# Batch 1's pooled queries and keys summed by unit-matrix products, its pooled values summed inside the products that use them: a fused attention and feed-forward kernel

## The chip, the cores and the metric

The kernel runs on one core of one Trainium2 chip. The metric is the device time of one execution in microseconds (us). Three runs of the kernel before gave 1031.43, 1028.47 and 1034.59, a median of 1031.43. Engines are named as in the profile: PE is TensorE (PEld its weight loads), DVE is VectorE, ACT is ScalarE, POOL is GpSimd, SP is SyncE, which here issues most DMA transfers.

## The reference

Queries, keys and values have 8 batches, 8 heads, 576 positions and a head size of 64. Two attentions are added, and a gated feed-forward layer follows. In short:

```python
q_d, k_d, v_d = (t.reshape(B, H, Sd, 4, D).mean(axis=3) for t in (q, k, v))   # Sd = 144
out_up = np.repeat(sm_attn(q_d, k_d, v_d), 4, axis=2)                         # pooled attention
mask = np.abs(pos[:, None] - pos[None, :]) < 4                                # local attention
out_local = softmax(where(mask, q @ k.T / sqrt(D), -1e9)) @ v
x = (out_up + out_local) as 4608 tokens x 512
h = x @ w_in                                                                   # 512 -> 2048
return (h * cos(h)) @ w_out                                                    # 2048 -> 512
```

The pooled attention needs sums over four neighbouring positions of queries, keys and values; the change concerns these sums.

## The kernel before, in words

**Units.** The attention of one batch and one pair of heads is a unit; there are 32, four per batch. A unit runs in five functions. `u_qk` loads queries and keys with the head dimension on the partitions (128 x 584) and sums four neighbouring positions into `qkd` (128 x 144 each): by one DVE reduction (line 480) or three POOL additions (lines 473 and 475). `u_v` loads the values, once as `vd4` (72 x 8 x 128, where the eight are two halves of the pooled keys times four neighbours) for the pooled attention and once as `vl` for the local one, and sums `vd4` over its four neighbours into `vd` by two additions (lines 494 and 495) on POOL or DVE. `u_s` makes the local scores (96 matmul records, line 518) and the pooled scores (line 526), and runs both softmaxes: masks and maxima on DVE (537, 542, 550), exponentials on ACT (562, 565), sums and reciprocals on DVE (577 to 581), scaling on DVE or POOL (583). `u_t` transposes the weights, the local ones on DVE (600), the pooled ones on PE (609), with a copy from the accumulator bank by ACT or DVE (`evac`, 455 and 456). `u_pv` multiplies by the values: the pooled product on PE (626), the local product on PE (637). DVE joins the two into `xs` (645), and the sum is split into a high and a low part, `xh` (660 or 661) and `xl` (389), which are the feed-forward layer's inputs.

**Feed-forward.** Tokens go in 12 tiles of 384. For each tile and each of 16 chunks of 128 hidden columns, `gemm1` does 12 matmuls (line 688), ACT and DVE apply the gate (697 to 705), and `gemm2` does 9 matmuls two steps later (line 724). The first three tiles go through the chunks four at a time; the others take all 16 in a row. Tile 0 holds tokens of batch 0 only. Tile 1 (`x1h`, `x1l`) holds the rest of batch 0 and a third of batch 1, so its first `gemm1` can start only when all four units of batch 1 are done.

**Weights.** They arrive as 64-bit numbers in two words and are turned into a high and a low part by `w_split`: ACT (410), four DVE steps (411, 413, 415, 417), ACT or DVE (421, 422) and a subtraction on POOL or DVE (389).

**Order.** No engine's order is written by hand. The functions record operations with a due time, a cost and the buffers that they read and write; `Plan.schedule` goes over them eight times with its own costs and writes one order per engine, which the hardware then follows strictly. Operations with alternatives (a reduction on DVE or POOL, a copy on ACT or DVE) are placed by the same pass. Where the plan sees a gap on PE in the first 300 us, the last loop fills it with matmuls of a bf16 unit matrix (line 841, `ident_b`) that compute nothing that is used. Any change of a cost or an operation therefore moves other operations too. The loads are chained in a fixed order on SP.

**Names.** `early` is a unit of batch 0 or 1 (`NEARLY = 2`). `ON_PE` is a tuple, empty before. `ident` is the fp32 unit matrix. `wxi`, `wxo`, `xxl` and `xxh` in the profile are areas of later weights and tiles, lent to the early units' buffers and to `w_split`.

Of the kernel before, what the change touches and what calls it, by code (L numbers as in the profile page):

```python
# [36 lines left out]
SD = S // 4  # L37
# [9 lines left out]
F64_TOP = float(np.uint32(0x47EFFFFF).view(np.float32))  # L47
NEG = -2.0 ** 100
NEARLY = 2
ON_PE = ()  # L50
BOOST = {0: 100.0}
LAG = 2
PI = math.pi
# [246 lines left out]
def attn_ffn_kernel(ctx: ExitStack, tc: tile.TileContext, qT, kT, vdn, vl, w_in, w_out, out):  # L300
# [79 lines left out]
    def dma(nbytes, fn, r=(), w=(), pw=()):  # L380
        o = pl.op("SP", max(0.45, nbytes / 262e3), fn, r=r, w=w, pw=pw, lat=1.8)
        loads.setdefault((pl.name,) + pl.arg, []).append(o)
        return o
# [63 lines left out]
    def bank(b, kind):  # L447

        if b == 0:
            tags = ("pa.0", "po.0", "pa.1", "po.1") if kind == "s" else ("ph.0", "ph.1", "pa.2")  # L450
            return psum(tags[int(pl.turn("early" + str(kind == "s"), len(tags))[-1])])
        return psum(pl.turn("pa", 3))
# [6 lines left out]
    def u_qk(b, pr):  # L459
        pl.name = "u_qk"  # L460
        q, k, qkd = (ub(b, pr, n) for n in ("q", "k", "qkd"))
        s4 = [lambda: q.get()[:, 0:S].rearrange("p (a r) -> p a r", r=4), lambda: k.get()[:, PAD:PAD + S].rearrange("p (a r) -> p a r", r=4)]
        early = b < NEARLY
        bk = bank(b, "t") if early and ON_PE else None
        for i, (src, ram) in enumerate(((q, qT), (k, kT))):
            dma(4 * P * SP_, lambda src=src, ram=ram: sp.dma_start(src.get(), ram[b, pr]), w=[src])

            def on_pe(i=i):
                for r in range(4):
                    pe.matmul(bk.get()[:, i * SD:(i + 1) * SD], ident, s4[i]()[:, :, r], start=(r == 0), stop=(r == 3))  # L470

            def on_pool(i=i):
                pool.tensor_tensor(out=qkd.get()[:, i], in0=s4[i]()[:, :, 0], in1=s4[i]()[:, :, 1], op=ALU.add)
                for r in (2, 3):
                    pool.tensor_tensor(out=qkd.get()[:, i], in0=qkd.get()[:, i], in1=s4[i]()[:, :, r], op=ALU.add)
            if early and i in ON_PE:
                pl.op("PE", 4 * _mm4(SD), on_pe, r=[src], pw=[bk])
                evac(SD, lambda i=i: qkd.get()[:, i], lambda i=i: bk.get()[:, i * SD:(i + 1) * SD], bk, qkd)
            else:
                pl.op("DVE", _dve(S), lambda i=i: dve.tensor_reduce(out=qkd.get()[:, i], in_=s4[i](), axis=AX.X, op=ALU.add),  # L480
                      r=[src], pw=[qkd], alts=[("POOL", 3 * _pool(2 * SD), on_pool)])
        st[(b, pr)] = dict(q=q, k=k, qkd=qkd)

    def u_v(b, pr):
        pl.name = "u_v"
        vd4, vt = ub(b, pr, "vd4"), ub(b, pr, "vl")
        dma(16 * P * HD * 2, lambda: sp.dma_start(vd4.get(), vdn[b, pr].rearrange("p a r n -> p (a r) n")), w=[vd4])
        dma(4 * P * 12 * D, lambda: sp.dma_start(vt.get(), vl[b, pr]), w=[vt])
        vd = ub(b, pr, "vd")
        v4 = lambda: vd4.get().rearrange("p (a r) n -> p a r n", a=2)  # L490

        def v_add(e):
            def f():
                e.tensor_tensor(out=v4()[:, :, 0:2, :], in0=v4()[:, :, 0:2, :], in1=v4()[:, :, 2:4, :], op=ALU.add)
                e.tensor_tensor(out=vd.get(), in0=v4()[:, :, 0, :], in1=v4()[:, :, 1, :], op=ALU.add)
            return f
        pl.op("POOL", 2.2, v_add(pool), w=[vd, vd4], alts=[("DVE", 1.1, v_add(dve))], shares=True)
        st[(b, pr)].update(vd=vd, vl=vt)
# [116 lines left out]
    def u_pv(b, pr):  # L615
        pl.name = "u_pv"
        u = st.pop((b, pr))
        ptl, ptd, vd, vt = (u[n] for n in ("ptl", "ptd", "vd", "vl"))
        xd, xs = ub(b, pr, "xd"), ub(b, pr, "xs")
        banks = [bank(b, "v") for _ in range(2)]  # L620
        poo, loc = pl.buf(None), [pl.buf(None) for _ in banks]

        def d_mm():
            for kh in range(2):
                for h in range(2):
                    pe.matmul(banks[0].get()[64 * h:64 * h + 64, 2 * SD:3 * SD], vd.get()[:, kh, 64 * h:64 * h + 64],  # L626
                              ptd.get()[:, h, kh, :], start=(kh == 0), stop=(kh == 1))
        pl.op("PE", 0.64, d_mm, r=[vd, ptd], pw=[banks[0]], w=[poo])

        def l_mm():  # L630
            for a in range(NSEG // 2):
                for i in range(4):
                    for e in range(2):
                        for h in range(2):
                            r = slice(64 * h + 32 * e, 64 * h + 32 * e + 32)
                            o = (4 * a + i) * BQ
                            pe.matmul(banks[e].get()[64 * h:64 * h + 64, o:o + BQ], vt.get()[r, a, i, :], ptl.get()[r, 4 * a + i, :BQ],  # L637
                                      start=True, stop=True)
        pl.op("PE", 1.52, l_mm, r=[vt, ptl], pw=banks, w=loc)

        evac(SD, xd.get, lambda: banks[0].get()[:, 2 * SD:3 * SD], banks[0], xd, scale=0.25)
        xd.w[-1].deps += poo.w
        half = [pl.buf(None) for _ in range(2)]
        for e in range(2):
            pl.op("DVE", _dve(S // 2), lambda e=e: dve.tensor_tensor(
                out=xs.get().rearrange("p (a e n r) -> p a e n r", e=2, a=NSEG // 2, r=4)[:, :, e],
                in0=banks[e].get()[:, :12 * BQ].rearrange("p (a n r) -> p a n r", a=NSEG // 2, r=4),
                in1=xd.get().rearrange("p (a e n) -> p a e n", e=2, a=NSEG // 2)[:, :, e].unsqueeze(3).broadcast_to(
                    [P, NSEG // 2, BQ, 4]), op=ALU.add), r=[banks[e], loc[e], xd], pw=[xs], w=[half[e]])
        lo = 0  # L650
        while lo < S:

            tt = tile_of(b * S + lo)
            to = min(S, FROM[tt] + SIZE[tt] - b * S)
            a, m = b * S + lo - FROM[tt], to - lo
            written[tt] += m
            done = pl.buf(None)
            hi = lambda tt=tt, a=a, m=m: x_tile(tt)[0][:, pr, a:a + m]
            src = lambda lo=lo, to=to: xs.get()[:, lo:to]
            pl.op("ACT", _act(m, False), lambda hi=hi, src=src: act.activation(hi(), src(), AF.Copy),  # L660
                  r=[xs], w=[done], pw=[x_b[tt]], alts=[("DVE", _dve(m / 2), lambda hi=hi, src=src: dve.tensor_copy(hi(), src()))])
            sub(m, lambda tt=tt, a=a, m=m: x_tile(tt)[1][:, pr, a:a + m], src, lambda hi=hi: hi().bitcast(F32),
                r=[xs, done], pw=[x_b[tt]])
            lo = to
# [214 lines left out]
```

## Time and profile before

| what | value |
|---|---|
| runs | 1031.43, 1028.47, 1034.59 us |
| profiled execution | 1031.63 us, of which the span from the first to the last instruction is 1029.5 us |
| PE, PEld, DVE, ACT, POOL busy | 97%, 84%, 66%, 59%, 22% of the span |
| granted TensorE clock, mean | 0.983 |
| filler matmuls (line 841) | 124, in the first 112 us |
| first `gemm1` of tile 0, of tile 1 | 53.29 us, 115.32 us |

The profile is read as follows. A timeline row gives the start, the length, the engine, the line, the operation, what is written from what, how many records follow each other, and in brackets the engine's idle time before it with what ended that. A row of the chain of waits gives start, length and the engine and line on the path that ended last. An fp32 matmul stands as two records in the trace, so that the four matmuls of line 526 appear as x8. Consecutive DVE rows overlap by some 0.07 us, so that one costs that much less than its length when it stands in line. `issue` is time in which an engine waited for nothing that the profile shows.

### The profile page before, as it was taken

How to read it: one execution, taken by the hardware profiler on the slowest of the kernel's cores; microseconds unless marked ns; L12 is line 12 of the kernel's file. 1: busy time of each engine (PE TensorE's matmuls, PEld its weight loads, DVE VectorE, ACT ScalarE, POOL GpSimd, SP SyncE). 2: the span in 40 equal slices, each digit the busy share in tenths (PEclk: the TensorE clock that was granted, in tenths of full speed). 3: DMA queues.
4: the chain of work that ended last, by engine and by line, in shares of the span. 5: the costliest groups of instructions: out<-in, count | busy, mean ns of one | idle time of the engine just before them, and what ended most of it. 6: DMA issues, size and time to landing. Idle time of an engine off the chain costs nothing.

```text
span 1029.5 us, 25935 instructions
## 1 busy us (share of the span) xinstructions
PE 1003.0 (97%) x11068; PEld 864.9 (84%) x11068; DVE 676.9 (66%) x1353; ACT 610.6 (59%) x1176; POOL 228.8 (22%) x274
## 2 busy tenths in 40 slices
PE   7889999999999999999999999999999999999998
PEld 4557788889988888889898888888888888899997
DVE  6699889996478668564738856755646865543443
ACT  2546577786566666565646655655655765655554
POOL 5596424433135201010103300101002410000000
PEclk8988899999999999999999999999999999999999
DMA  9762751434245312100202401200101310000000
GB/s 265 237 221 85 242 183 46 61 59 62 32 106 144 76 50 75 59 25 28 76 6 76 133 28 38 96 25 28 55 27 43 120 51 1 32 1 1 31 1 31
DMA packets 36450, 76.11 MB, mean 74 GB/s; under 512 B 3440, under 2 KB 11632, under 8 KB 36336
## 3 DMA queue, kind: packets, MB, share of 16 engines
q1 hardware_dynamic: 32448, 67.38, 20.6%
q0 software_dynamic: 3888, 7.08, 5.0%
q8 instruction: 87, 1.43, 0.6%
q14 instruction: 27, 0.22, 0.1%
HBM read 57.93 MB, written 16.52 MB: 72 GB/s over the span
## 4 chain that ended last, share of the span: by engine, by line
PE 81%; DVE 10%; DMA 4%; ACT 2%; issue 2%; POOL 0%; SPq 0%; ACTq 0%; DVEq 0%; POOLq 0%
PE bank L688 35%; PE bank L724 35%; PE bank L637 3%; PE bank L518 3%; PE bank L526 2%; DMA q<-qT 2%; PE bank L609 2%; DMA wdi<-w_in 1%; PE bank L626 1%; DVE su L577 1%; DVE qkd L480 1%; DVE mxd L550 1%; PE bank L841 1%; DVE gl L389 1%; DVE tr L700 1%
## 5 line engine op out<-in xcount | busy, mean ns | idle before, releaser
L724 PE MATMUL bank<-wo,gh 128*128 128x512 f32 x1152 | 363.3, 396 | 0.0
L724 PEld LDWEIGHTS bank<-wo,gh 128*128 128x128 f32 x1152 | 210.0, 188 | 35.8 <-issue 2.3
L724 PE MATMUL bank<-wo,gl 128*128 128x512 f32 x576 | 228.0, 396 | 0.6 <-POOL su L535 0.6
L699 ACT ACTIVATE tr<-bank,bmagic 128x384 f32<-128x384 f32 x192 | 111.0, 579 | 134.0 <-PE bank L688 122.5
L703 DVE SCALAR_TENSOR_TENSOR tr<-tr,bank 128x384 f32<-128x384 f32 x192 | 105.3, 549 | 121.7 <-ACT tr L698 121.4
L700 DVE SCALAR_TENSOR_TENSOR tr<-tr,bank 128x384 f32<-128x384 f32 x192 | 105.5, 550 | 97.5 <-ACT tr L699 97.3
L697 ACT ACTIVATE tr<-tr 128x384 f32<-128x384 f32 x192 | 100.7, 524 | 84.4 <-DVE tr L700 83.7
L705 ACT ACTIVATE gh<-tr 128x384 fp32r<-128x384 f32 x177 | 92.5, 523 | 90.7 <-DVE tr L703 89.0
L389 DVE TENSOR_TENSOR gl<-tr,gh 128x384 fp32r<-128x384 f32 x160 | 97.3, 609 | 68.6 <-ACT gh L705 67.2
L724 PEld LDWEIGHTS bank<-wo,gl 128*128 128x128 f32 x576 | 108.0, 187 | 24.8 <-POOL su L535 1.0
L688 PE MATMUL bank<-x0h,wi 128*128 128x384 f32 x384 | 109.9, 347 | 0.7 <-DVE tr L703 0.7
L688 PE MATMUL bank<-x1h,wi 128*128 128x384 f32 x384 | 107.6, 341 | 0.0
L688 PE MATMUL bank<-x2h,wi 128*128 128x384 f32 x384 | 107.1, 339 | 0.0
L688 PE MATMUL bank<-x3h,wi 128*128 128x384 f32 x384 | 106.9, 339 | 0.0
L389 POOL TENSOR_TENSOR gl<-tr,gh 128x384 fp32r<-128x384 f32 x32 | 38.1, 1189 | 301.3 <-DVE gh L706 215.8
L698 ACT ACTIVATE tr<-tr 128x384 f32<-128x384 f32 x192 | 100.8, 525 | 6.1
L688 PEld LDWEIGHTS bank<-x0h,wi 128*128 128x128 f32 x384 | 72.1, 193 | 3.7 <-DVE tr L703 0.8
L688 PEld LDWEIGHTS bank<-x1h,wi 128*128 128x128 f32 x384 | 70.7, 189 | 2.9 <-issue 0.8
L688 PEld LDWEIGHTS bank<-x2h,wi 128*128 128x128 f32 x384 | 70.2, 188 | 2.8 <-DVE sml L537 0.6
L688 PEld LDWEIGHTS bank<-x3h,wi 128*128 128x128 f32 x384 | 70.2, 188 | 2.5 <-issue 0.6
L688 PE MATMUL bank<-x0l,wi 128*128 128x384 f32 x192 | 65.8, 342 | 0.0
L688 PE MATMUL bank<-x3l,wi 128*128 128x384 f32 x192 | 64.6, 336 | 0.5 <-POOL x3l L389 0.5
(192 smaller groups left out, 1473.0 us busy)
## 6 DMA issues: line engine op xcount, KB each, us to landing
vl<-vl SPq DMA_DIRECT2D x26, 384.0 KB
out<-ob SPq DMA_DIRECT2D x36, 256.0 KB
wdi<-w_in SPq DMA_DIRECT2D x16, 512.0 KB
wdo<-w_out SPq DMA_DIRECT2D x16, 512.0 KB
q<-qT SPq DMA_DIRECT2D x26, 292.0 KB
k<-kT SPq DMA_DIRECT2D x26, 292.0 KB
vd<-vdn SPq DMA_DIRECT2D x26, 288.0 KB
out<-ob POOLq DMA_DIRECT2D x27, 256.0 KB, 5.7
```

Of the source, the lines that this page charges most:

```text
L389: f = lambda e: lambda: e.tensor_tensor(out=out(), in0=in0(), in1=in1(), op=ALU.subtract)
L518: pe.matmul(banks[n // NSEG].get()[64 * h + BS * e:64 * h + BS * (e + 1), c:c + BS], q.get()[hs, o:o + BS], k.get()[hs, o:o + BS], start=T ...
L526: pe.matmul(banks[h].get()[:HD, i * SD:(i + 1) * SD], qkd.get()[hs, 0, i * HD:(i + 1) * HD], qkd.get()[hs, 1, :], start=True, stop=True)
L637: pe.matmul(banks[e].get()[64 * h:64 * h + 64, o:o + BQ], vt.get()[r, a, i, :], ptl.get()[r, 4 * a + i, :BQ], start=True, stop=True)
L688: pe.matmul(ph.get()[:, :m], w[:, i, kc, :], x[:, kc, :], start=(n == 0), stop=(n == 3 * KC - 1))
L697: act.activation(tr.get(), tr.get(), AF.Sin, scale=PI)
L698: act.activation(tr.get(), tr.get(), AF.Square)
L699: pl.op("ACT", _act(m, True, 1), lambda: act.activation(tr.get(), h(), AF.Identity, bias=bmagic), r=[ph], w=[tr])
L700: pl.op("DVE", _dve(m), lambda: dve.scalar_tensor_tensor(out=tr.get(), in0=tr.get(), scalar=MAGIC, in1=h(), op0=ALU.subtract, op1=ALU.subt ...
L703: pl.op("DVE", _dve(m), lambda: dve.scalar_tensor_tensor(out=tr.get(), in0=tr.get(), scalar=0.5, in1=h(), op0=ALU.subtract, op1=ALU.mult), ...
L705: pl.op("ACT", _act(m, False), lambda: act.activation(gh.get(), tr.get(), AF.Copy), r=[tr], w=[gh], alts=[("DVE", _dve(m / 2), lambda: dve ...
L724: pe.matmul(o, (gh, gh, gl)[k].get()[:, sl], wo.get()[:, (0, 1, 0)[k]], start=(c == c0 and k == 0), stop=(c == c1 - 1 and k == 2))
```

## The change

`ON_PE` becomes `(1,)` and now names batches. For the four units of batch 1:

- `u_qk` sums queries and keys on PE: four fp32 matmuls each with the stationary unit matrix and, as moving operand, every fourth position (`s4[i]()[:, :, r]`, a step of four elements), accumulated in a bank. Then `evac` copies the 128 x 144 result to `qkd`. Per unit that is 8 matmuls and two copies for two reductions (or six POOL additions).
- `u_v` ends after its loads; nothing sums the values. `u_pv` multiplies all eight slices of `vd4` instead of the two of `vd`, 16 matmuls in place of 4, each half of the weights used for its four neighbours. `vd4` stays in use until that product.

```diff
-ON_PE = ()
+ON_PE = (1,)
...
-        bk = bank(b, "t") if early and ON_PE else None
+        on = early and b in ON_PE
+        bk = bank(b, "t") if on else None
...
             def on_pe(i=i):
                 for r in range(4):
                     pe.matmul(bk.get()[:, i * SD:(i + 1) * SD], ident, s4[i]()[:, :, r], start=(r == 0), stop=(r == 3))
...
-            if early and i in ON_PE:
+            if on:
                 pl.op("PE", 4 * _mm4(SD), on_pe, r=[src], pw=[bk])
                 evac(SD, lambda i=i: qkd.get()[:, i], lambda i=i: bk.get()[:, i * SD:(i + 1) * SD], bk, qkd)
             else:
...
         dma(4 * P * 12 * D, lambda: sp.dma_start(vt.get(), vl[b, pr]), w=[vt])
+        if b in ON_PE:
+            st[(b, pr)].update(vd=vd4, vl=vt)
+            return
...
         def d_mm():
-            for kh in range(2):
+            n = 8 if b in ON_PE else 2
+            for j in range(n):
                 for h in range(2):
-                    pe.matmul(banks[0].get()[64 * h:64 * h + 64, 2 * SD:3 * SD], vd.get()[:, kh, 64 * h:64 * h + 64],
-                              ptd.get()[:, h, kh, :], start=(kh == 0), stop=(kh == 1))
-        pl.op("PE", 0.64, d_mm, r=[vd, ptd], pw=[banks[0]], w=[poo])
+                    pe.matmul(banks[0].get()[64 * h:64 * h + 64, 2 * SD:3 * SD], vd.get()[:, j, 64 * h:64 * h + 64],
+                              ptd.get()[:, h, j * 2 // n, :], start=(j == 0), stop=(j == n - 1))
+        pl.op("PE", 2.56 if b in ON_PE else 0.64, d_mm, r=[vd, ptd], pw=[banks[0]], w=[poo])
```

The planner's new order differs on every engine. The changed file is a few lines longer, so the same code has other numbers there: 471 is the unit product (470 before), 481 the reduction (480), 522 and 530 the local and pooled scores (518, 526), 546, 554 and 581 the maxima and sums (542, 550, 577), 613 the transposes on PE (609), 631 and 642 the pooled and local value products (626, 637), 693 and 729 the two feed-forward products (688, 724), 846 the filler (841); lines up to 455 are unchanged. Below, the changed numbers stand in the rows of the change; the text uses those of before.

The first place is PE from the pooled product of batch 0's third unit to the first `gemm1`. Before, with the filler rows left out where the dots stand:

```order
L626 MATMUL bank<-wxi_194 64x144 x4
...
L637 MATMUL bank<-wxo_384,wxi_496 64x24 x48
...
L609 MATMUL bank<-ident,wxi_208 72x72 x4
L518 MATMUL bank<-k,q 32x32 x48
...
L637 MATMUL bank<-wxi_550,wxo_579 64x24 x48
...
L626 MATMUL bank<-wxo_267 64x144 x4
...
L526 MATMUL bank<-qkd 72x144 x4
L688 MATMUL bank<-x0h,wi_936 128x384
```

The same place in the change (`xxl`, `wxo_787`, `wxi_799`, `wxo_826` and `wxo_841` are queries and keys of batch 1's other three units):

```order
L631 MATMUL bank<-wxi_194 64x144 x4
L471 MATMUL bank<-q,ident 128x144 x4
L471 MATMUL bank<-k,ident 128x144 x4
...
L613 MATMUL bank<-ident,wxi_208 72x72 x4
L471 MATMUL bank<-xxl,ident 128x144 x4
...
L471 MATMUL bank<-wxo_826,ident 128x144 x4
...
L631 MATMUL bank<-wxo_267 64x144 x4
...
L642 MATMUL bank<-wxi_544,wxo_579 64x24 x48
L471 MATMUL bank<-wxo_841,ident 128x144 x4
```

Seven of the eight groups of unit products now stand ahead of the last products of batch 0's fourth unit, the eighth behind them; the two score products of batch 1's first unit follow, and then two `gemm1` in a row (one before).

The second place is DVE in the softmax of batch 1's first unit, from the subtraction of the maximum to the sums. Before:

```order
L389 TENSOR_TENSOR sml<-sml,mxl 128x384
L480 TENSOR_REDUCE wxi_126<-xxl 128x144
L480 TENSOR_REDUCE wxo_191<-wxi_853 128x144
L494 TENSOR_TENSOR vd_969<-vd_969 72x2x256
L495 TENSOR_TENSOR vd<-vd_969 72x256
L577 TENSOR_REDUCE su<-sml 128x12
```

In the change (`wdo_673` and `wdi_849` are words of weights under conversion):

```order
L389 TENSOR_TENSOR sml<-sml,mxl 128x384
L417 SCALAR_TENSOR_TENSOR xxh<-wdo_673,xxh 128x512
L415 SCALAR_TENSOR_TENSOR xxh<-wdi_849,xxh 128x512
L422 CAST wo_1060<-xxh 128x512
L417 SCALAR_TENSOR_TENSOR xxh<-wdi_849,xxh 128x512
L411 TENSOR_SCALAR xxh<-xxh 128x512
L581 TENSOR_REDUCE su<-sml 128x12
```

The place of the sums of queries, keys and values is taken by steps of weight conversion that stood later before.

The third place is PE behind that softmax. Before:

```order
L609 MATMUL bank<-ident,smd 72x72 x8
L518 MATMUL bank<-xxl 32x32 x48
L526 MATMUL bank<-wxi_126 72x144 x4
L626 MATMUL bank<-ptd,vd 64x144 x4
...
L637 MATMUL bank<-ptl,vl 64x24 x48
...
L609 MATMUL bank<-ident,wxi_126 72x72 x8
```

In the change (of the `gemm1` and `gemm2` between, the first row of each is shown):

```order
L613 MATMUL bank<-ident,smd 72x72 x8
...
L522 MATMUL bank<-xxl 32x32 x48
L530 MATMUL bank<-wxi_126 72x144 x4
L631 MATMUL bank<-ptd,vd_934 64x144 x16
L693 MATMUL bank<-x0h,wi_1069 128x384
...
L729 MATMUL bank<-wo_865,gh 128x512 x2
...
L642 MATMUL bank<-ptl,vl 64x24 x48
L693 MATMUL bank<-x0h,wi_1314 128x384
...
L613 MATMUL bank<-ident,wxi_126 72x72 x4
```

Two `gemm1` and one `gemm2` of tile 0 have moved ahead of the second unit's transposes. The whole order holds 100 fillers, 24 fewer; up to tile 1's first `gemm1` both orders hold the same units, four `gemm1` and two `gemm2`. The two copies of each unit of batch 1 stand on ACT. The order of the loads on SP is the same there.

## Prediction

> **What bounds the kernel now.** I read the page, then busy time by stretches cut at three events on PE (the transposes of batch 0's third unit at 36.49, tile 0's first `gemm1` at 53.29, tile 1's first `gemm1` at 115.32), then the chain of waits and the timelines. The page gives the engines' shares:
>
> ```profile
> span 1029.5 us, 25935 instructions
> PE 1003.0 (97%) x11068; PEld 864.9 (84%) x11068; DVE 676.9 (66%) x1353; ACT 610.6 (59%) x1176; POOL 228.8 (22%) x274
> ```
>
> The stretches show length, each engine's busy time, granted clock and DMA; below them, the fillers alone in the second and third stretch:
>
> ```profile
> 36.49:53.29 16.80, 14.27 (x351) 8.73 (x351) 10.87 (x20) 6.43 (x16) 9.92 (x13) 0.90 0.44 127
> 53.29:115.32 62.03, 53.67 (x986) 37.38 (x984) 56.71 (x110) 32.85 (x90) 44.14 (x47) 0.82 0.53 174
> 115.32:200.00 84.68, 84.10 (x519) 75.47 (x518) 76.66 (x141) 62.75 (x118) 34.52 (x34) 0.99 0.43 124
> 200.00:1024.24 824.24, 821.48 (x8528) 726.72 (x8527) 508.25 (x1030) 492.42 (x897) 121.07 (x139) 1.00 0.19 50
> ```
>
> ```profile
> 36.49:53.29 16.80, 7.41 (x22) 1.98 (x22) 0.90 0.44 127
> 53.29:115.32 62.03, 15.31 (x53) 5.12 (x53) 0.82 0.53 174
> ```
>
> Behind 115.32 PE idles 0.6 + 2.8 us in 909: it is the bound, and its work there is the same in both orders. So the end moves with tile 1's first `gemm1`, one for one, and the forecast is a forecast of that event. Ahead of it PE is no bound: of 78.8 us in the second and third stretch 22.7 are fillers and 10.9 idle, while DVE is busy for 56.7 of the third stretch's 62.0.
>
> What paces the second stretch, A, is PE's own order (timeline of PE):
>
> ```profile
> 39.26 1.59 PE L637 MATMUL bank<-wxo,wxi 32*64 32x24 f32 x96
> 41.58 1.02 PE L518 MATMUL bank<-k,q 64*32 64x32 f32 x96
> 42.97 0.41 PE L609 MATMUL bank<-ident,wxi 72*72 72x72 f32 x4
> 43.75 1.13 PE L637 MATMUL bank<-wxi,wxo 32*64 32x24 f32 x64
> 47.41 0.66 PE L637 MATMUL bank<-wxi,wxo 32*64 32x24 f32 x32 [2.53 <-issue]
> 48.53 1.04 PE L626 MATMUL bank<-wxo 72*64 72x144 f32 x8
> 52.64 0.71 PE L526 MATMUL bank<-qkd 64*72 64x144 f32 x8
> ```
>
> From the end of the third unit's local product (40.85) to the end of the fourth unit's pooled one (49.57) PE issues one thing after another, with one unexplained stop of 2.53. `gemm1` follows the scores at 53.29.
>
> The third stretch goes in four rounds, one for each unit of batch 1: scores (526), softmax on DVE and ACT, transposes (609), then the next unit's scores:
>
> ```profile
> 61.26 0.67 PE L609 MATMUL bank<-ident,smd 72*72 72x72 f32 x8 [2.37 <-DVE smd L583]
> 63.01 1.24 PE L526 MATMUL bank<-wxi 64*72 64x144 f32 x8
> 74.46 0.78 PE L609 MATMUL bank<-ident,wxi 72*72 72x72 f32 x8 [1.75 <-DVE wxi L583]
> 76.17 1.24 PE L526 MATMUL bank<-wxo 64*72 64x144 f32 x8
> 89.73 0.67 PE L609 MATMUL bank<-ident,wxo 72*72 72x72 f32 x4 [2.10 <-DVE wxo L583]
> 94.74 0.71 PE L526 MATMUL bank<-wxi 64*72 64x144 f32 x8
> 105.42 0.69 PE L609 MATMUL bank<-ident,wxi 72*72 72x72 f32 x8
> 115.32 0.69 PE L688 MATMUL bank<-x1h,wi 128*128 128x384 f32 x1
> ```
>
> From the end of 526 to the start of 609 the rounds take 7.9, 10.2, 12.3 and 10.0 us; DVE's line 583 ends the wait three times. Between the rounds PE needs 3.0, 3.0 and 5.7 us, and 9.9 from the last transposes to tile 1.
>
> Half clock makes some of this longer: the same four matmuls of 526 take 0.71 or 1.24, and the twelve of `gemm1` 2.10 or 4.36 (chain of waits; L724 is `gemm2`):
>
> ```profile
> 78.57 4.36 PE bank L688 x12
> 90.40 3.45 PE bank L688 x12
> 118.44 2.08 PE bank L724 x9
> 120.53 2.10 PE bank L688 x12
> ```
>
> The long rows stand behind the idle ends of 1.75 to 2.37 in the rows above.
>
> **The change part by part.** *Added on PE.* The nearest row to a unit product is 526 at full clock: four fp32 matmuls over 144 columns, eight records, in 0.71, two at a time on halves of the rows. The unit product uses all rows, so nothing runs beside it: its eight steps lie between 1.0 and 1.3, and as groups follow each other and only the last has a fixed end, I take 1.0, 8.0 for eight. The pooled value product keeps its pairs: four times the steps and one end, 2.1 instead of 0.7, 5.6 more for four units. That is 13.6 us on an engine with 33.6 us of filler and idle in the two stretches, and the order holds 24 fillers less, 5 to 7 us at 15.31 / 53 each. So most of it is covered by slots that computed nothing; where PE paces (stretch A), it costs.
>
> *Stretch A.* From the third unit's pooled product on, PE now has two groups, the fourth unit's transposes, five groups, then pooled and local product. The third unit's two products change places and end at about 40.9. Up to `gemm1` then follow eight groups 8.0, four pairs of fillers 2.0, transposes 0.5, pooled 0.7, local 1.6, and the scores 1.0 + 0.7: 14.5, so that `gemm1` stands at 55.4 instead of 53.29. **+2.1.** This leaves out the stop of 2.53, of which no row tells the cause; if it comes back, +4.6. If groups overlap as 526 does (0.65), -0.7.
>
> The operand of these products steps over every fourth word. No PE row has such an operand: POOL, which reads the same words, is no measure for PE; the bounds are no cost and, for a word fetched at half the rate, 2.0 a group. I take no cost, since an fp32 column already takes PE 1.0 / (4 x 144) = 1.7 ns. [...]
>
> *Removed from DVE and POOL.* DVE and POOL rows in the rounds:
>
> ```profile
> 53.39 0.68 POOL L473 TENSOR_TENSOR wxi<-xxl 128x144 f32<-128x144 f32 x1
> 70.79 1.06 POOL L495 TENSOR_TENSOR wxo<-wxi 72x256 f32<-72x256 f32 x1
> 55.76 0.74 DVE L480 TENSOR_REDUCE wxi<-xxl 128x144 f32<-128x576 f32 x1
> 58.02 0.68 DVE L495 TENSOR_TENSOR vd<-vd 72x256 f32<-72x256 f32 x1
> 55.29 0.54 DVE L389 TENSOR_TENSOR sml<-sml,mxl 128x384 f32<-128x384 f32 x1
> 61.51 0.41 DVE L411 TENSOR_SCALAR xxh<-xxh 128x512 f32<-128x512 f32 x1
> 60.38 0.73 DVE L583 TENSOR_TENSOR smd<-smd,su 72x576 f32<-72x576 f32 x1
> 66.70 1.75 DVE L415 SCALAR_TENSOR_TENSOR xxh<-wdo,xxh 128x512 int32<-128x512 int32 x1
> 69.51 1.75 DVE L417 SCALAR_TENSOR_TENSOR xxh<-wdo,xxh 128x512 int32<-128x512 int32 x1
> 76.36 0.64 DVE L415 SCALAR_TENSOR_TENSOR xxh<-wdi,xxh 128x512 int32<-128x512 int32 x1
> 86.81 2.78 DVE L583 TENSOR_TENSOR wxo<-wxo,su 72x576 f32<-72x576 f32 x1
> ```
>
> From 53.39 to 71.85 POOL does nothing but the sums of batch 1, apart from memsets: 18.5 of its 44.1 us in the third stretch go. DVE loses four instructions, 55.76 to 58.63, 2.9 us.
>
> DVE does not stand idle for that; the order gives it weight conversion. Round by round, counting what stands between 526 and 583 beside the softmax itself, at 0.6 for 415 and 417, 0.33 for 411 and 413, 0.47 for a 384-wide step (the rows above less their overlap): round 1 loses 3.9 and gains 4.1; round 2 goes from 3.1 to 4.9; round 3 from 3.9 to 5.5; round 4 from 5.6 to 4.3. **+2.3**, with work that was done later before.
>
> Against that stands contention. A step of 0.64 took 1.75 twice, and 583 took 2.78 instead of 0.73, each while POOL worked: 4.3 us in three rows, some 8 with the smaller ones of rounds 2 and 3. With over 40% of POOL's work gone, and that in the very rounds, I take **-4.5** (from -2 to -8).
>
> *Between the rounds.* PE does two `gemm1`, a `gemm2` and the longer value product between the first and second transposes: 2.1 x 2 at half clock, 2.1 x 2, 2.1 and 1.6, together 12.1 against some 9.6 for DVE's round, so that it comes about 2.5 late there; the `gemm1` of 3.45 between the third and fourth is gone in return. Sum -0.5. Round 4 loses half a microsecond behind fillers before (105.42): **-1.0** in all.
>
> *The last part* took 9.9: transposes, pooled and local product, join, split, with a stop and half clock. Now: transposes 0.7, waiting for DVE's transposition 0.8, local 1.6, pooled 2.1, fillers 0.9, next scores 1.7: 7.8. **-2.1**, none of it if the clock drops again.
>
> *Moved to ACT.* Eight copies of 128 x 144:
>
> ```profile
> L455 ACT ACTIVATE wxi<-bank 128x144 f32<-128x144 f32 x3 | 0.9, 291 | 7.9 <-PE bank L626 5.4 <-PE bank L637 2.5
> ```
>
> 8 x 0.29 = 2.3 us on an engine busy for 32.85 of 62.03: covered. Behind a late copy stand the fourth unit's pooled product (the same bank) and batch 1's scores, at 0.3 each if ACT is caught in a conversion. `vd4` of the first unit is freed later, at its product instead of at 58.7; the load of batch 2's values waits for it on SP, with `vl` behind it, which waited for line 637 anyway. Nothing.
>
> Sum: 2.1 + 2.3 - 4.5 - 1.0 - 2.1 = -3.2; tile 1 at 112.1. The profiled execution took 1031.63, 2.1 more than its span and 0.2 above the median, so 1031.6 - 3.2 = **1028.4**.
>
> **The rivals.** *Stretch A outweighs the rest (slower).* If a group costs 2.0, for the operand's step, eight cost 8 more in a place where PE paces, and the stop of 2.53 comes back behind the same 96-record product: 1028.4 + 8 + 2.5 = 1038.9. It decides from 1.75 a group with the stop (1028.4 + 6 + 2.5 = 1036.9). For it: PE issues without a break there. Against: fp32 columns are slow already. [...]
>
> *Contention all but vanishes (much faster).* DVE saves 8 instead of 4.5, and fewer idle ends spare a slow spell (4.36 - 2.10 = 2.3): 1028.4 - 3.5 - 2.3 = 1022.6. For it: the long rows lie where POOL is busiest. Against: 25 us of POOL work stay.
>
> *It moves nothing.* DVE's freed time goes into conversion, and PE's longer queue ahead of the second transposes eats the rest (2.5, doubled at half clock): tile 1 at 115, 1031. The clock is the open part: idle ends of 1.75 to 2.37 were enough for half clock before, and such ends remain. [...]
>
> **How the numbers follow.** The forecast has 0.50 (its own range 1025 to 1031.5), much faster 0.25, nothing 0.13, slower 0.12. About 0.5%, 5.2 us, can be told from no change here: faster is below 1026.4, slower above 1036.8. Of the forecast 0.15 lies below 1026.4, so faster 0.15 + 0.25 = 0.40; slower 0.10, as a little of that rival falls short; no change 0.50. The range runs from 1021.5, just below the much faster case, to 1036, near 1035.5, where the ends of A (+4.6), of contention (-2) and of the last part (0) meet; about 0.16 lies outside.
>
> **What would show it.** A group of unit products spans 1.0 and tile 0's first `gemm1` starts at 55 to 56; the rounds no longer hold DVE rows of 1.75 or 2.78; POOL is busy for some 25 us in them; tile 1's first `gemm1` is at 111 to 112; behind it PE idles some 3 us as before. The prediction is wrong if groups take 1.6 or more, if that `gemm1` is outside 106 to 119, or if the end does not move with it.

## The result, and the profile after

The changed kernel ran in 1046.85 us (three runs, 1043.47 to 1049.83), 1.0145 times the time before, with a 95% interval of 1.0113 to 1.0176: some 15 us slower, where 3 us faster was forecast. The profiled execution, the fastest of the three, took 1043.47, 2.1 more than its span. One execution of a kernel tried below, the changed one with fillers, took 1410.53 us at a mean clock of 0.647; it stands in no ratio. The head of the page of the changed kernel:

```profile
span 1041.4 us, 26189 instructions
PE 1019.3 (98%) x11204; PEld 880.6 (85%) x11204; DVE 671.8 (65%) x1348; ACT 611.2 (59%) x1185; POOL 206.6 (20%) x250
```

The stretches, cut at the first `gemm1` of tile 0 and of tile 1 (length, busy time of PE, PEld, DVE, ACT and POOL with counts, granted clock, DMA share, GB/s):

```profile
0.00:68.87 68.87, 62.02 (x1091) 39.74 (x1091) 37.68 (x84) 23.77 (x79) 24.33 (x50) 0.85 0.58 187
68.87:125.74 56.87, 50.74 (x1070) 38.88 (x1068) 54.72 (x114) 36.10 (x94) 26.69 (x26) 0.94 0.58 190
125.74:1025.00 899.26, 894.97 (x8994) 792.16 (x8993) 575.51 (x1144) 544.90 (x1000) 155.54 (x175) 1.00 0.21 57
```

Tile 1's first `gemm1` came at 125.74 instead of 115.32. Behind it the span goes on for 915.7 us (1041.4 - 125.74), before for 914.2, and PE idles 4.3 of the 899: the end moved with that event, as the prediction had it, but for 1.5 us. The loss is ahead of tile 0's `gemm1`, at 68.87 instead of 53.29. The PE timeline there (lines 471, 530, 631, 642 and 693 were 470, 526, 626, 637 and 688):

```profile
25.47 2.09 PE L642 MATMUL bank<-ptl,vl 32*64 32x24 f32 x79 [2.07 <-issue]
33.63 2.77 PE L642 MATMUL bank<-wxi,wxo 32*64 32x24 f32 x96
44.73 0.71 PE L631 MATMUL bank<-wxi 72*64 72x144 f32 x8
51.55 2.24 PE L471 MATMUL bank<-xxl,ident 128*128 128x144 f32 x8
53.61 2.22 PE L471 MATMUL bank<-wxo,ident 128*128 128x144 f32 x8
55.66 2.23 PE L471 MATMUL bank<-xxl,ident 128*128 128x144 f32 x8
68.87 0.45 PE L693 MATMUL bank<-x0h,wi 128*128 128x384 f32 x1
```

Two things are to be seen. A group of unit products takes 2.05 us from start to start, at full clock, not 1.0. And batch 0's third unit, whose products had ended at 40.9 (39.26 + 1.59), ends at 45.4 (44.73 + 0.71): behind a stop of 2.07 at 25.47 the clock was at half (0.50 from 25.8 to 42.9), so that the 96 records of the local product took 2.77 instead of 1.59.

The third stretch, by contrast, took 56.87 at a clock of 0.94 (before 62.03 at 0.82), and the prediction had 56.7 (55.4 to 112.1). Its PE rows:

```profile
77.18 0.67 PE L613 MATMUL bank<-ident,smd 72*72 72x72 f32 x8 [2.13 <-DVE smd L587]
79.91 2.18 PE L631 MATMUL bank<-ptd,vd 72*64 72x144 f32 x32
90.51 0.41 PE L613 MATMUL bank<-ident,wxi 72*72 72x72 f32 x4
104.26 0.79 PE L613 MATMUL bank<-ident,wxo 72*72 72x72 f32 x8 [1.83 <-DVE wxo L587]
115.43 0.67 PE L613 MATMUL bank<-ident,wxi 72*72 72x72 f32 x8 [1.61 <-DVE wxi L587]
117.94 4.10 PE L631 MATMUL bank<-wxo,wxi 72*64 72x144 f32 x32
```

The longer value product has its forecast 2.1 us (2.18), and 4.10 at half clock. DVE's longest rows in this stretch are now these, against 1.75 and 2.78 before; POOL is busy for 26.7 us of it, where some 25 were forecast:

```profile
86.91 1.70 DVE L389 TENSOR_TENSOR wi<-xxh,wi 128x512 fp32r<-128x512 f32 x1
88.97 1.39 DVE L587 TENSOR_TENSOR wxi<-wxi,su 72x576 f32<-72x576 f32 x1
```

So the first reading is: a unit product costs twice what was forecast, and the rest was right. The experiments confirm the first half and not the second.

### The profile page after: what moved, and what is told of

Its sections match the earlier page's. It is cut to its first block, busy times and chain, and to the rows that moved or that the text cites. A ratio compares the mean times of both kernels' runs of the same rounds, so it can differ in the third digit from the quotient of the medians.

```text
span 1041.4 us, 26189 instructions
## 1 busy us (share of the span) xinstructions
PE 1019.3 (98%) x11204; PEld 880.6 (85%) x11204; DVE 671.8 (65%) x1348; ACT 611.2 (59%) x1185; POOL 206.6 (20%) x250
## 4 chain that ended last, share of the span: by engine, by line
PE 86%; DVE 7%; ACT 2%; POOL 2%; DMA 2%; issue 1%; SPq 0%; ACTq 0%; DVEq 0%; POOLq 0%
PE bank L693 36%; PE bank L729 36%; PE bank L642 4%; PE bank L522 2%; PE bank L631 2%; PE bank L530 2%; PE bank L471 2%; PE bank L846 2%; PE bank L613 2%; DMA k<-kT 1%; DVE su L581 1%; POOL qkd L476 1%; DVE qkd L481 1%; DMA wxo<-kT 1%; DVE xs L650 0%
## 5 line engine op out<-in xcount | busy, mean ns | idle before, releaser
L389 DVE TENSOR_TENSOR gl<-tr,gh 128x384 fp32r<-128x384 f32 x158 | 95.2, 603 | 69.3 <-ACT gh L710 68.2
L693 PE MATMUL bank<-x0h,wi 128*128 128x384 f32 x384 | 107.1, 340 | 0.1
L693 PE MATMUL bank<-x2l,wi 128*128 128x384 f32 x192 | 64.5, 336 | 0.0
```

Of the source, the lines that this page charges most:

```text
L389: f = lambda e: lambda: e.tensor_tensor(out=out(), in0=in0(), in1=in1(), op=ALU.subtract)
L693: pe.matmul(ph.get()[:, :m], w[:, i, kc, :], x[:, kc, :], start=(n == 0), stop=(n == 3 * KC - 1))
```

## The experiments

Three questions: why a group costs 2.05, what the change would have done at 1.0, and what takes the difference between that and the forecast. All ratios are to the kernel before on the same chip, with 95% intervals.

**What doubles the group.** Either the moving operand's step of four words, or the fp32 matmul of two records with a full 128 x 128 stationary operand, which no row of before had. The first kernel takes the step away:

```diff
-            def on_pe(i=i):
+            def on_pe(i=i, src=src):
                 for r in range(4):
-                    pe.matmul(bk.get()[:, i * SD:(i + 1) * SD], ident, s4[i]()[:, :, r], start=(r == 0), stop=(r == 3))
+                    pe.matmul(bk.get()[:, i * SD:(i + 1) * SD], ident, src.get()[:, r * SD:(r + 1) * SD], start=(r == 0), stop=(r == 3))
```

> The unit products read four blocks of 144 neighbouring words instead of every fourth word; order, shapes and counts are those of the changed kernel (the sums are of other positions, so this part of the computation is not the reference's). Theory 'step' (the moving operand's step of four words halves PE's rate): a record goes from 0.256 to 0.12-0.13 us, a group of eight from 2.05 to about 1.0, tile 0's first gemm1 from 68.9 to 60 or 61, the time by 6 to 8 to 1037-1041. Theory 'whole array' (an fp32 matmul with a 128 x 128 stationary operand takes 0.256 a record, since its weight load is not hidden): unchanged, 2.05 a group, gemm1 at 68-69, 1043-1050. If the half clock from 25.8 to 42.9 is a matter of the single execution and not of the change, gemm1 comes 4 us earlier in either case.

Ratio 1.0077 (1.0044 to 1.0109). Its PE timeline and stretches:

```profile
45.41 1.14 PE L471 MATMUL bank<-wxo,ident 128*128 128x144 f32 x8
46.39 1.14 PE L471 MATMUL bank<-xxl,ident 128*128 128x144 f32 x8
47.37 1.14 PE L471 MATMUL bank<-wxi,ident 128*128 128x144 f32 x8
55.34 0.44 PE L693 MATMUL bank<-x0h,wi 128*128 128x384 f32 x1
63.65 0.67 PE L613 MATMUL bank<-ident,smd 72*72 72x72 f32 x8 [2.13 <-DVE smd L587]
67.14 4.11 PE L631 MATMUL bank<-ptd,vd 72*64 72x144 f32 x32
80.95 0.41 PE L613 MATMUL bank<-ident,wxi 72*72 72x72 f32 x4
117.18 0.44 PE L693 MATMUL bank<-x1h,wi 128*128 128x384 f32 x1
```

```profile
55.34:117.18 61.84, 55.95 (x1069) 43.86 (x1068) 53.95 (x114) 36.64 (x94) 23.45 (x26) 0.83 0.53 175
```

A group takes 0.98, and tile 0's `gemm1` starts at 55.34; the prediction had 1.0 and 55.4. The second kernel keeps the step and does each product on the two quarters of the array that the unit matrix fills:

```diff
-                    pe.matmul(bk.get()[:, i * SD:(i + 1) * SD], ident, s4[i]()[:, :, r], start=(r == 0), stop=(r == 3))
+                    for h in (slice(0, 64), slice(64, P)):
+                        pe.matmul(bk.get()[h, i * SD:(i + 1) * SD], ident[h, h], s4[i]()[h, :, r], start=(r == 0), stop=(r == 3))
```

> Each unit product becomes two on the quarters of the array that the unit matrix fills (rows 0-63 to columns 0-63, 64-127 to 64-127), with the step of four words kept; the planner's order is that of the changed kernel. Theory 'step': two records side by side still take 0.25 us, a group (16 records) about 2.05 or more, gemm1 of tile 0 at 68-69, 1043-1050. Theory 'whole array': a pair takes 0.12-0.13 as in the scores, a group about 1.0, gemm1 at 60-61, 1037-1041.

Ratio 1.0135 (1.0091 to 1.018). Two of its groups (line 472 in this kernel) and tile 0's first `gemm1` (694):

```profile
48.33 2.23 PE L472 MATMUL bank<-wxo,ident 64*64 64x144 f32 x16
50.38 2.23 PE L472 MATMUL bank<-xxl,ident 64*64 64x144 f32 x16
63.63 0.44 PE L694 MATMUL bank<-x0h,wi 128*128 128x384 f32 x1
```

Still 2.05, with a quarter of the stationary operand in each product: it is the step. In this execution the clock stayed full from 24.0 to 71.8, and tile 0's `gemm1` came at 63.63, in the same order 8.3 us behind the 55.34 of neighbouring columns: that is the price of the step in time (8 x 1.07 = 8.6), without the half clock of the changed kernel's profile. How the price grows, a third kernel shows, with steps of 1, 2, 3 and 4 words in the four products of a group:

```diff
+            def on_pe(i=i, src=src):
+                o = bk.get()[:, i * SD:(i + 1) * SD]
+                pe.matmul(o, ident, src.get()[:, 0:SD], start=True, stop=False)
+                pe.matmul(o, ident, src.get()[:, 0:2 * SD:2], start=False, stop=False)
+                pe.matmul(o, ident, src.get()[:, 0:3 * SD:3], start=False, stop=False)
+                pe.matmul(o, ident, src.get()[:, 0:4 * SD:4], start=False, stop=True)
```

> Each unit product takes its four moving operands with steps of 1, 2, 3 and 4 words, on a line each (the sums are of other positions). [...] If any step breaks the full rate: 0.256 at 2, 3 and 4. Time 1037-1045.

Lines 471 to 474 are the steps 1 to 4, two records each; the price is the distance from start to start:

```profile
58.61 0.43 PE L471 MATMUL bank<-xxl,ident 128*128 128x144 f32 x2
58.87 0.42 PE L472 MATMUL bank<-xxl,ident 128*128 128x144 f32 x2
59.13 0.54 PE L473 MATMUL bank<-xxl,ident 128*128 128x144 f32 x2
59.50 0.68 PE L474 MATMUL bank<-xxl,ident 128*128 128x144 f32 x2
60.01 0.43 PE L471 MATMUL bank<-wxi,ident 128*128 128x144 f32 x2
```

0.26, 0.26, 0.37 and 0.51. Step 2 is free, against my expectation; from there the price follows the words swept. An estimate from the row of step 4: its two records sweep 2 x 576 words in 0.51, 0.44 ns a word; by that step 3, with 2 x 432, takes 0.38 (measured 0.37), and step 2, with 2 x 288, takes 0.26, as measured. Step 1, with 2 x 144, would take 0.13 and took 0.26 as well: below step 2 the price falls no further. Why it grows with the words no run shows. This execution took 1049.5, a single one, in which the clock was low from 28 to 55 (0.971 over the whole span).

**Does the planner make it worse?** It reckons with 0.97 a group.

```diff
-                pl.op("PE", 4 * _mm4(SD), on_pe, r=[src], pw=[bk])
+                pl.op("PE", 2.1, on_pe, r=[src], pw=[bk])
```

> The changed kernel with the unit product's planned cost at 2.1 us a group instead of 0.97, as measured; the planner places everything anew. If the loss is a matter of where a planner that believes 0.97 puts the groups: some groups move into idle stretches of PE, 1036-1042. If PE simply has to do 16 us of groups ahead of the rounds: 1043-1050 as before.

Ratio 1.0162 (1.0138 to 1.0186), against 1.0145: no. With the true price it finds no better place.

**Each part alone.** The values alone (`on = False`, nothing else):

> Only the second part of the change: the values' sums inside the pooled value products; the sums of queries and keys on DVE and POOL as before. If the loss lies in the unit products alone: gemm1 of tile 0 at 53-57, tile 1's at 112-117, 1026-1034. If the longer value products (2.1 instead of 0.7 us, in the chain between the rounds) lose as well: tile 1 at 118 or later, 1035 or more.

Ratio 0.9994 (0.9967 to 1.0022), tile 0 at 54.51, tile 1 at 117.52. No gain, no loss: the loss lies with the sums of queries and keys. These alone, with the step and with neighbouring columns (the early return in `u_v` removed, the pooled product back at two blocks):

> Only the first part of the change: the sums of queries and keys by PE, the values' sums on DVE and POOL as before. If the loss lies in the unit products alone: gemm1 of tile 0 at 64-69, tile 1's at 124-129, 1041-1050. If it takes both parts together: 1030-1038.

> The sums of queries and keys alone at the forecast price (neighbouring columns, 1.0 us a group), the values' sums on DVE and POOL as before. With the step it was 1.0194 against 1.0145 for both parts, so the value part took 0.5% off beside the sums: 1038-1041, ratio 1.010-1.012. If that gain hangs on the step: 1034-1036.

Ratios 1.0194 (1.0157 to 1.0232) and 1.0141 (1.0105 to 1.0177). Beside the sums, then, the value part seems worth about half a per cent (1.0194 against 1.0145, 1.0141 against 1.0077; within each pair the intervals overlap), though alone it is worth nothing. The third stretch of the second of these:

```profile
60.14:126.78 66.64, 51.88 (x985) 35.84 (x984) 61.47 (x117) 37.80 (x98) 34.38 (x34) 0.85 0.59 196
```

DVE is busy for 61.5 of 66.6 us, with 117 instructions against 110 before: the sums of queries and keys have left it and more has come in than left. What of it the rounds wait for is not shown; of the value sums, two rows with 2.6 us stand on DVE there.

**What is left at 1.0 a group.** The kernel with neighbouring columns is still 0.8% slower than before where the prediction had 0.3% faster, and its third stretch took 61.84 instead of 56.7, at a clock of 0.83: from the first to the second transposes 17.3 us (63.65 to 80.95) instead of 13.3, with a value product of 4.11 in between (in the changed kernel 77.18 to 90.51, with 2.18). First the clock. Eight fillers more ahead of the transposes of each unit of batch 1, where PE idles for 1.6 to 2.1 us:

```diff
+                if s and o.name == "u_t" and o.arg[0] == 1 and o.arg not in warmed:
+                    warmed.append(o.arg)
+                    n = max(n, 0) + 8
```

in the changed kernel, in the kernel before, with neighbouring columns, and with the values alone:

> The changed kernel with eight more filler matmuls ahead of each of the four transposes of batch 1, in the idle ends of 1.6 to 2.1 us that stand there. Theory 'half clock eats the gain' (idle ends in the rounds bring the clock down for 3.4 to 14 us each): the third stretch keeps full clock, tile 1 moves by 2 to 5 us ahead, 1040-1044. Rival 'the clock is not what counts': the fillers only take 1.8 us where PE is late already (second transposes), 1046-1049.

> The kernel before with the same eight fillers ahead of each of the four transposes. Its third stretch has the clock at half for 22 of 62 us. Theory 'half clock': third stretch at 56-59 instead of 62, 1025-1028. Rival: nothing or a loss of 1-2 us, 1029-1033.

> The kernel of e1_contig (neighbouring columns summed, 1.0 us a group) with eight fillers more ahead of each of the four transposes of batch 1. Theory 'half clock in the rounds is most of what is left': 1029-1032, ratio to before 1.000-1.003. Rival 'conversions on DVE are': 1034-1036, 1.005-1.008 as without the fillers.

> Only the second part of the change (the values' sums inside the pooled products) with the eight fillers ahead of each transposition of batch 1. Part two alone had the time of the kernel before with the clock at half for 20 of 63 us in the third stretch. If half clock on the longer products ate its gain: third stretch at 57-59, 1024-1028. If not: 1029-1033.

The ratios: 1.0077 (1.0046 to 1.0107) instead of 1.0145 for the changed kernel; 1.0013 (0.9997 to 1.0029) for the one before; 1.0039 (1.0014 to 1.0063) instead of 1.0077 with neighbouring columns; 1.0023 (1.0000 to 1.0047) for the values alone, whose profiled execution, the slowest of its ten, also waited 4.19 us for a load of weights ahead of the last value product. The fillers help clearly in the changed kernel alone; with neighbouring columns the intervals overlap. The third stretches of the first three (changed kernel, before, neighbouring columns; of the last also what stands ahead):

```profile
66.91:124.17 57.26, 54.69 (x1101) 39.70 (x1100) 53.82 (x114) 36.46 (x94) 25.99 (x26) 1.00 0.57 189
```

```profile
53.41:112.91 59.50, 55.00 (x1017) 36.85 (x1015) 55.39 (x106) 32.22 (x89) 44.15 (x47) 0.94 0.54 181
```

```profile
0.00:58.58 58.58, 51.18 (x1092) 33.24 (x1092) 37.93 (x84) 23.71 (x79) 24.11 (x50) 0.85 0.71 220
58.58:114.99 56.41, 54.58 (x1102) 39.71 (x1100) 53.52 (x114) 36.59 (x94) 25.98 (x26) 1.00 0.57 192
```

For the whole change in one order, the rounds are sorted by their clock: 56.4, 57.3 and 56.9 (the changed kernel) at 0.94 to 1.00; 61.8 and, with quarters, 63.2 at 0.83 and 0.78. The 5 us between the changed kernel and neighbouring columns lie, but for 0.9, between the first and the second transposes (13.33 and 17.30), where PE comes late at half clock; at three of the four transposes PE waits for DVE in both. The profile of the changed kernel does not show where its fillers gain, as its third stretch was at high clock already (56.87 without them, 57.26 with); that they gain by the clock is read from the runs, whose mean clocks are 0.979 to 0.986 without and 0.992 to 0.996 with them. A kernel with neighbouring columns and a value product of two blocks only shows the same from the other side:

```diff
-            for j in range(n):
+            for j in range(0, n, n // 2):
...
-                              ptd.get()[:, h, j * 2 // n, :], start=(j == 0), stop=(j == n - 1))
+                              ptd.get()[:, h, j * 2 // n, :], start=(j == 0), stop=(j == n // 2))
```

> The kernel of e1_contig (unit products at 1.0 us a group) whose pooled value product takes two of its eight value blocks: four matmuls, 0.7 us at full clock, with the planned cost and so the order kept. It leaves out the other six blocks, and adds neighbouring columns of queries and keys as e1_contig does. Theory 'PE comes late in the rounds' (in e1_contig the second transposes follow the first after 17.3 us, 13.2 before, with a value product of 4.11 among what lies between): the gap falls to 13-14, tile 1's first gemm1 from 117.2 to 112-114, 1030-1032. Rival 'DVE paces the rounds': tile 1 within a microsecond of e1_contig's, 1034-1037.

Its third stretch:

```profile
61.38:118.97 57.59, 51.32 (x973) 37.39 (x971) 54.73 (x114) 36.53 (x94) 23.55 (x26) 0.79 0.56 188
```

57.6 us in spite of a clock of 0.79: without the long product, half clock cost the rounds little in this execution. Tile 1 came no sooner all the same (118.97), since the clock had been at half from 26.6 to 43.7 and tile 0 was late; the ratio of 1.0046 (1.0016 to 1.0075) lies below 1.0077 with overlapping intervals.

Then DVE. Conversions of later chunks are held, in the planner, until batch 1's last softmax, with neighbouring columns; then the same with the fillers; then both in the changed kernel with its step:

```diff
+HELD = 4
...
+    gate = [o for o in pl.ops if o.name == "u_s" and o.arg == (1, NPAIR - 1)][-1]
+    for o in pl.ops:
+        if o.name == "w_split" and o.arg[1] >= HELD:
+            o.sdeps.append(gate)
```

> The kernel of e1_contig (1.0 us a group, neighbouring columns summed) with the weight conversions of chunks 4 and later held, in the planner, until the last softmax of batch 1 is done. In e1_contig and in the changed kernel DVE does three conversions more ahead of tile 1 than before (13 against 10, about 8 us). Theory 'the planner refills DVE with conversions that are not due': the rounds fall from 61.8 to 55-58, tile 1 at 111-114, 1029-1032. Rival 'half clock and PE's longer product pace the rounds': tile 1 at 116-118, 1034-1037.

> e10_hold with eight filler matmuls more ahead of the four transposes of batch 1, so that both suspected causes are taken away: conversions that are not due, and half clock behind idle ends. If these two and the step of four words are the whole loss: third stretch at 53-56, tile 1 at 109-112, 1025-1029, the prediction's own number. If something else is left: 1031 or more.

> The changed kernel, with its step of four words, conversions of chunks 4 and later held until the last softmax of batch 1, and the fillers. If the three causes add up (with neighbouring columns the same kernel had 1.0018): 8 groups dearer by 1.07 us, 1039-1042, ratio 1.008-1.011. If late groups are covered once the rounds are shorter: 1033-1036.

Ratios 1.0036 (0.9999 to 1.0072), 1.0018 (0.9989 to 1.0048) and 1.0099 (1.0061 to 1.0137). The first one's third stretch:

```profile
59.59:119.41 59.82, 52.93 (x1058) 41.78 (x1057) 50.84 (x107) 33.82 (x89) 17.04 (x21) 0.83 0.52 172
```

DVE has 3 us less to do and idles for 9 of 59.8. At the same clock of 0.83 the stretch is 2.0 us shorter than the 61.84 with neighbouring columns alone; that theory's 55 to 58 did not come, so the conversions were at most a part of what the rounds waited for. The time is lower, by an amount within the intervals. With the fillers too the third stretch took 58.7 (neighbouring columns) and 59.9 (the step) at clocks of 0.94 and 0.92, no shorter than the 56.4 to 57.3 without holding. The other two differ in the step alone: 1.0099 against 1.0018, 0.8%. Two more pairs do so, with the fillers 1.0077 against 1.0039 and with the sums alone 1.0194 against 1.0141; with 1.0145 against 1.0077 the step costs 0.4 to 0.8%, 4 to 8 us, in four pairs. At a group price of 1.0, both remedies together come back to the kernel before, and not below it.

Last, one step of four in each product, with neighbouring columns:

```diff
-                for r in range(4):
-                    pe.matmul(bk.get()[:, i * SD:(i + 1) * SD], ident, src.get()[:, r * SD:(r + 1) * SD], start=(r == 0), stop=(r == 3))
+                for r in range(1):
+                    pe.matmul(bk.get()[:, i * SD:(i + 1) * SD], ident, src.get()[:, 0:SD], start=True, stop=True)
```

> The kernel of e1_contig with one step of four in each unit product (it leaves out three quarters of those sums): eight groups at 0.25 instead of 0.98, planned cost and order kept. Stretch A ends 5 to 6 us earlier, tile 0's first gemm1 at 49-51. Theory 'the end moves with it one for one', as the prediction had it: tile 1 at 111-112, 1029-1031. Rival 'the rounds have their own pace': they take longer by what A is shorter, tile 1 at 115-117, 1033-1036.

Ratio 1.0069 (1.0045 to 1.0093): 6 us of work less on PE, and no gain that can be told. Neither theory had this. Its profiled execution, the slowest of its six, shows where it can go:

```profile
19.99 1.39 PE L522 MATMUL bank<-wxo,wxi 64*32 64x32 f32 x85 [3.49 <-issue]
29.02 1.56 PE L642 MATMUL bank<-ptl,vl 32*64 32x24 f32 x79 [3.30 <-issue]
36.66 2.77 PE L642 MATMUL bank<-wxi,wxo 32*64 32x24 f32 x96
49.21 1.23 PE L631 MATMUL bank<-wxi 72*64 72x144 f32 x8
```

Behind a stop of 3.30 at the very place where the changed kernel stopped for 2.07, the clock stayed at half from 30.0 to 57.3, and tile 0 started at 63.64; its third stretch took 62.6 at a clock of 0.81. The other five runs had low clocks too, 0.977 to 0.983, where neighbouring columns had 0.979 to 0.990. Whether the end would follow A one for one under an even clock this kernel does not tell.

## Why the prediction was wrong, point by point

**The price of a unit product: the step that failed.** Stretch A was put together rightly; at 1.0 a group it ends where forecast (55.34 against 55.4). But a group costs 2.05, 8 x 1.07 = 8.6 us more, and by the four pairs of runs 0.4 to 0.8%. I had the bound, 2.0, an estimate of mine (twice 1.0), and took no cost, since an fp32 column takes 1.7 ns anyway (two records). That reasoning covers a step of two (0.26, the same as none), and not one of four (0.51). The rival "Stretch A outweighs the rest" is what happened; its stop of 2.53 did not come back in A.

**The clock: left out of the sum.** The rival's 1038.9 fell 8 us short, because the rest of the sum did not hold either: at 1.0 a group the ratio is 1.0077, not 0.997. The prediction called the clock "the open part" and gave it no term. It shows in two places. In the rounds the products that the change makes longer can stand at half clock (4.11 instead of 2.18), and the fillers there take 0.7% off the changed kernel. And ahead of A, the pooled product of batch 0's third unit ended at 45.4 where I had 40.9; with neighbouring columns in the same order, without half clock there, it ended at 40.4. That second place belongs to the execution and not to the order. In profiles whose order ahead of tile 0 is the same, the clock was at half between 24 us and A for 0, 10.2 and 17.1 us, and tile 0's `gemm1` came at 55.34, 58.58 and 61.37 with neighbouring columns (alone, with fillers, with two value blocks) and at 63.63, 66.92 and 68.87 with the step (quarters, fillers, the changed kernel).

Yet the clock is not the whole rest. The seven runs with neighbouring columns have a mean clock of 0.984, those of the kernel before on the same chip 0.985; among the seven, 0.01 less goes with some 9.5 us more, so that the difference is worth about 1 us of 7 or 8. The changed kernel's three runs have 0.983, by the same estimate 2 to 3 us of 15. The kernel before pays for half clock nearly as much. What remains is that the gain did not come: at a price of 1.0 tile 0 was 2.05 later, as forecast, the third stretch 0.2 shorter at equal clock where 5.3 was forecast, and the time behind it 1.9 longer. The rival "It moves nothing" comes nearest to that, with tile 1 at 115 (measured 117.18) and PE's longer queue doubled at half clock. What takes the 1.0039 with fillers was not traced further.

**Contention, conversions and rounds.** The forecast of 56.7 for the third stretch was met at high clock (56.4 to 57.3), but for a reason only half right, and that the changed kernel's own profile met it was luck of its clock. Compared at like clock the gain was 2.6 (59.50 before with fillers and 56.87, both at 0.94) and 0.2 (62.03 at 0.82 and 61.84 at 0.83), of the 5.3 forecast; 2.5 is what the fillers took off the kernel before (62.03 to 59.50). The long DVE rows went, as forecast (1.70 and 1.39 are the longest left). But the row of 2.78 before, from 86.81 to 89.59, stood for most of its time beside these rows of POOL, a scaling and a weight subtraction; that it went because of the sums is not shown:

```profile
86.93 0.83 POOL L583 TENSOR_TENSOR wxo<-wxo,su 128x384 f32<-128x384 f32 x1
87.72 1.26 POOL L389 TENSOR_TENSOR wi<-xxh,wi 128x512 fp32r<-128x512 f32 x1
```

DVE's busy time fell by 2.0 only, from 56.71 to 54.72, with 114 instructions in place of 110: the conversion steps of lines 411 to 417 are 36 there where they were 33, the subtractions of line 389 13 in place of 10.

**Between the rounds and the last part.** From tile 0's `gemm1` over the four transposes to tile 1's `gemm1`:

| kernel | to 1st | to 2nd | to 3rd | to 4th | to tile 1 |
|---|---|---|---|---|---|
| before | 7.97 | 13.20 | 15.27 | 15.69 | 9.90 |
| changed | 8.31 | 13.33 | 13.75 | 11.17 | 10.31 |
| neighbouring columns | 8.31 | 17.30 | 13.83 | 12.09 | 10.31 |

The gain is in the third and fourth round. "PE comes about 2.5 late" at the second transposes was right in kind: no wait stands at 90.51. At half clock it is 4 us more. The last part was forecast at 7.8 and took 10.31 in both: the clock dropped again (0.67 over it in the changed kernel, at half from 118.0 on), and the sentence "none of it if the clock drops again" applied; at full clock, with fillers, it took 9.1 in the changed kernel and 8.2 with neighbouring columns.

**The foundation.** That the end moves with tile 1's `gemm1` held to within 2 us: behind it 914.2 us before, 915.7 after, 916.1 with neighbouring columns. Beside a forecast gain of 3.2 that is not nothing.

## What to carry to other kernels

Price a new operand by its access pattern, not by the nearest instruction's name: find a row with the same step, or estimate the cost from the words swept (0.44 ns each here, from a step of two on), and when no row supports the cheaper of two bounds, give the dearer one a place in the sum. Before counting a stretch's waits as gain, compare its clock: about half of the gain forecast in the rounds was half clock in the one profiled execution of before. And work that is lengthened behind an idle end of PE may be paid at half clock: the same value product took 2.18 in one execution and 4.11 in another.

## What the runs showed of the hardware

- An fp32 matmul of 144 columns with a 128 x 128 unit matrix takes 0.26 us at a step of one or two words of the moving operand, 0.37 at three, 0.51 at four, and the same 0.51 on quarters of the array.
- The stops of PE that end with "issue" stand at fixed counts. Of the records of PE and PEld and their waits for semaphores, the following stood ahead of them: 450, 706, 1986 and 4034 before; 450, 706 and 961 after; 450, 706, 961 and 1474 with neighbouring columns; 4289 in others. These are 194 + 256 n within one record. How long a stop is changes from run to run: at 961 all fourteen kernels that have sums on PE stop, for 0.22 to 3.75 us. The two profiles of the kernel before and of that kernel with fillers have none there, and one of 2.53 at 1986, the stop that the prediction could not explain. What decides the length stays open.
- The half clock ahead of A goes with that stop. In the eight of the fourteen profiles where it took 1.02 us or more, a spell of half clock of 6.8 to 27.3 us began within it or at most 2.4 us behind it; in the four where it took 0.58 or less, none began there; of the two between, 0.76 had one behind it and 0.92 had none for 14 us. Whether the stop causes the spell no run tests.
- In the changed kernel an idle end of 2.13 us at the first transposes left the clock at full; with neighbouring columns the same idle end, 2.13 us at the same place, was followed by 10 us at half. The length of the idle time alone does not decide it.
